# A gated mix of attention and a feed-forward block: the input loaded plainly and turned on TensorE, and more zero products

## The chip, the cores and the metric

The kernel runs on one core of a Trainium2 chip. The metric is the device time of one execution in microseconds; the kernel before takes 845.47 us, the median of three runs (844.47 to 847.02). Engines are named as in the profile: PE is TensorE, DVE is VectorE, ACT is ScalarE, POOL is GpSimd, SP is the engine whose queue issues most transfers.

## The reference

The input x is 2048 rows of 512 columns in bfloat16. A gate g is computed for each row; the output mixes an attention block with 32 heads of 16 columns and a feed-forward block of width 1792.

```python
x = A_x                                            # (1, 2048, 512)
g = sigmoid((x * gate_w).sum(-1, keepdims=True))
# a: multi-head attention without a mask
qkv = (x @ A_wqkv)                                 # 32 heads, 16 columns each
p = softmax(q @ k.T * 16 ** -0.5)
a = (p @ v) @ A_wo
# b: feed-forward
b = (silu(x @ B_w_gate) * (x @ B_w_up)) @ B_w_down
return g * a + (1 - g) * b
```

Each product contracts over the 512 columns of x, and TensorE contracts over partitions. So the kernel needs x with its columns on the partitions: the tile `xT`, 128 partitions by 4 column blocks (`dc`) by 2048 rows.

## The kernel before

The kernel has a prologue and a body. The prologue brings in x and the first weights and makes the keys, queries and a bound on the scores for the first four heads (group 0). The body runs 32 units (4 blocks of 512 queries times 8 groups of 4 heads), and each unit goes over 16 blocks of 128 keys: scores on TensorE into PSUM (`s_t`), exponentials on ScalarE (`e_t`), products with the values on TensorE (`o_ps`). A part of the exponentials (`d_t`, `y_t`, `z_t`, `u_t`) is computed on VectorE instead. The feed-forward pieces and the remaining projections are put between the scores by a planner that runs when the kernel is built. It keeps estimated clocks for the engines (`plan.pe`, `plan.dve`, `plan.act`) and fixes the order of instructions on each engine.

The load of x, in two halves of rows and four column blocks, by transfers that transpose:

```python
xT = big.tile([P, DC, S], BF16, name="xT")
for t0 in (0, 2 * QBW):                            # QBW = 512
    for dc in range(DC):                           # DC = 4
        nc.sync.dma_start_transpose(out=xT[:, dc, t0:t0 + 2 * QBW],
                                    in_=x[t0:t0 + 2 * QBW, dc * P:(dc + 1) * P])
# ... the small weight slices for group 0 on ScalarE's queue, the rest of wqkv behind x on SP's
```

The prologue proper. `keep_warm` multiplies a zero tile, so that TensorE is active while it waits for data; `k0` makes keys of group 0, `v0` values, `qp0` holds queries, `largest` takes the largest magnitude of a row (for the bound), and `k0_evict` moves the keys to SBUF:

```python
keep_warm(14)
for dc in range(DC):
    for tb in range(2):
        k0(dc, tb)
    mm(qp0[:, :], lhsT=wpad[0][:, dc, :], rhs=xT[:, dc, 0:QBW], ...)
    if dc < DC - 1:
        keep_warm(2)
largest(0, kp0[0][:, :])
act(out=q0r[:, :], in_=qp0[:, :], func=ACT.Copy)
act(out=aq0[:, :], in_=qp0[:, :], func=ACT.Abs)
vec.tensor_scalar(out=kneg1, ...)                  # bound step
for v in range(2):
    vec.tensor_scalar(out=q0[0][:, v, :], in0=q0r[:, :], ...)
k0_evict(0)
for dc in range(DC - 1):
    for tb in (2, 3):
        k0(dc, tb)
    if dc == 0:
        v0(0)
    else:
        keep_warm(3)
# ... the last k0 of each block, largest(1), largest(2), two bound steps (kneg0)
k0_evict(1)
v0(8)
mm(bp0[:, :], lhsT=kneg0, rhs=aq0[:, :], start=True, stop=True)
for v in range(2):                                 # queries with their bound; then the first scores
    vec.scalar_tensor_tensor(out=q0[0][:, v, :], in0=bp0[:, :], ...)
```

In the body, where the planner sees that TensorE would have to wait for a score bank, it first tries real work. If there is none, more than 0.4 us is left, and little work was planned in the last 3 us, it puts in four zero products, which add zeros to the accumulator that is open:

```python
if room > 0.4 and closed in o_of and 0 < pvs[closed] < KT - 1 and sum(
        w for t, w in work_at[-24:] if t > plan.pe - 3.0) < 6.5:
    for j in range(4):
        mm(o_of[closed][32 * j:32 * j + 16, :], lhsT=vaug[:, 0, G * 4 * VC:],   # a block of zeros
           rhs=xT[:, 0, 0:QBW], start=False, stop=False, tile_position=(0, 32 * j), ...)
    spend("C", 1)
    continue
```

Of the kernel before, what the change touches and what calls it, by code (L numbers as in the profile page):

```python
# [78 lines left out]
def kernel(  # L79
# [12 lines left out]
    nc = tc.nc  # L92
    P = 128
    x = A_x.flatten_outer_dims()
    S, D = x.shape
# [34 lines left out]
    const = ctx.enter_context(tc.tile_pool(name="const", bufs=1))  # L130
    big = ctx.enter_context(tc.tile_pool(name="big", bufs=1))
# [7 lines left out]
    ps_o = ctx.enter_context(tc.tile_pool(name="ps_o", bufs=1, space=bass.MemoryType.PSUM))  # L139
    ps_m = [ctx.enter_context(tc.tile_pool(name=f"ps_m{i}", bufs=1, space=bass.MemoryType.PSUM)) for i in range(3)]  # L140
# [15 lines left out]
    def mm(*args, **kw):  # L156
        return ordered(nc.tensor.matmul(*args, **kw))  # L157

    def act(*args, **kw):
        ordered(nc.scalar.activation(*args, **kw))  # L160
# [7 lines left out]
    vec = Ordered()  # L168


    xT = big.tile([P, DC, S], BF16, name="xT")
    for t0 in (0, 2 * QBW):
        for dc in range(DC):
            nc.sync.dma_start_transpose(out=xT[:, dc, t0:t0 + 2 * QBW], in_=x[t0:t0 + 2 * QBW, dc * P:(dc + 1) * P])
    wqk = big.tile([P, DC, 2 * D], BF16, name="wqk")
    for c0 in (D, 0):

        nc.scalar.dma_start(out=wqk[:, :, c0:c0 + 64],
                            in_=A_wqkv[:, c0:c0 + 64].rearrange("(dc p) c -> p dc c", p=P))
# [6 lines left out]
    for c0 in (D, 0):  # L186
        nc.sync.dma_start(out=wqk[:, :, c0 + 64:c0 + D],
                          in_=A_wqkv[:, c0 + 64:c0 + D].rearrange("(dc p) c -> p dc c", p=P))
# [1 line left out]
    wo_t = big.tile([P, NB, D], BF16, name="wo_t")  # L190

    wo_l = big.tile([P, 2, D], BF16, name="wo_l")
    wd_t = big.tile([P, FC, D], BF16, name="wd_t")

    def late_loads():
        nc.sync.dma_start(out=gw_col[:], in_=gate_w.rearrange("(dc p) -> p dc", p=P))
# [9 lines left out]

    kaug = big.tile([P, G, S], BF16, name="kaug")

    mt = big.tile([P, FC, QBW], BF16, name="mt")
    idle = mt[:, 4, :]  # L210
    nc.vector.memset(idle, 0.0)
    wpad = [mt[:, i, :].rearrange("p (dc c) -> p dc c", c=P) for i in range(2)]
# [7 lines left out]
    vsel = const.tile([P, 2], F32, name="vsel")  # L220
# [3 lines left out]
    bsel0 = mt[:, 3, 0:P]  # L224
# [3 lines left out]
    for i in (1, 0):  # L228
        nc.vector.tensor_copy(
            out=wpad[i][:, :, :].rearrange("p dc (j c) -> p dc j c", c=32)[:, :, :, 1:1 + DH],  # L230
            in_=wqk[:, :, i * D:i * D + 64].rearrange("p dc (j c) -> p dc j c", c=DH))
    def ones_rows(engine, g):

        engine.memset(kaug[:, g, :].bitcast(F32), 1.0019378662109375)
    for g in range(1, 4):
        ones_rows(nc.vector, g)
    vaug = big.tile([P, KT, G * 4 * VC + 16], BF16, name="vaug")
    nc.gpsimd.memset(vaug[:, :, G * 4 * VC:], 0.0)

# [20 lines left out]
    nc.gpsimd.memset(sel_t[:], 0.0)  # L260
    for j in range(4):
        nc.gpsimd.memset(sel_t[32 * j:32 * j + 1, j:j + 1], 1.0)
    ident = const.tile([P, P], BF16, name="ident")
    nc.gpsimd.memset(ident[:], 1.0)
    nc.gpsimd.affine_select(out=ident[:], in_=ident[:], pattern=[[-1, P]], compare_op=ALU.is_equal,
                            fill=0.0, base=0, channel_multiplier=1)

    kb = const.tile([P, NB], F32, name="kb")
    kneg = const.tile([P, NB, 8], BF16, name="kneg")
# [13 lines left out]
    plan = Plan()  # L283
    owed = []
    work_at = []
# [157 lines left out]
    def v0(t0):  # L443

        p = m_tile("vp")
        for i in range(8):
            for dc in range(DC):
                mm(p[:, 64 * i:64 * i + 64], lhsT=xT[:, dc, (t0 + i) * P:(t0 + i + 1) * P], rhs=wv[:, dc, 0:64],
                   start=(dc == 0), stop=(dc == DC - 1))
        act(out=vaug[:, t0:t0 + 8, 0:4 * VC].rearrange("p t (h c) -> p t h c", c=VC)[:, :, :, 1:1 + DH],  # L450
            in_=p[:, :].rearrange("p (t h c) -> p t h c", h=4, c=DH), func=ACT.Copy)
        m_free(p, 0.0)
# [26 lines left out]
    q1 = big.tile([P, 2, QBW], BF16, name="q1")  # L479
    nc.gpsimd.memset(q1[:], 0.0)  # L480
    nc.gpsimd.memset(qx[0][:], 0.0)
    for g in range(5, G):
        ones_rows(nc.gpsimd, g)

    q0 = [(qx[1][:, :, :, :], on_t[0][:, :, :].rearrange("p (v i) q -> p v i q", v=2))[qb // 2][:, :, qb % 2, :]
          for qb in range(QB)]
# [479 lines left out]
    kp0 = [ps_s.tile([P, 2 * QBW], F32, tag="s", name="kp0") for _ in range(2)]  # L966
    qp0 = m_tile("qp0")
# [15 lines left out]
    kneg1 = mt[:, 3, 2 * P:3 * P]  # L983

    def largest(i, ps):
        vec.tensor_reduce(out=kpart0[:, i:i + 1], in_=ps, axis=AX.X, op=ALU.max, apply_absolute_value=True)

    def k0_evict(i):
        act(out=kaug[:, 0, i * 2 * QBW:(i + 1) * 2 * QBW], in_=kp0[i][:, :], func=ACT.Identity,
            bias=onescol[:, 0:1], scale=1.0)  # L990

    keep_warm(14)
    for dc in range(DC):
        for tb in range(2):
            k0(dc, tb)
        mm(qp0[:, :], lhsT=wpad[0][:, dc, :], rhs=xT[:, dc, 0:QBW], start=(dc == 0), stop=(dc == DC - 1))
        if dc < DC - 1:
            keep_warm(2)
    largest(0, kp0[0][:, :])
    act(out=q0r[:, :], in_=qp0[:, :], func=ACT.Copy)  # L1000
    act(out=aq0[:, :], in_=qp0[:, :], func=ACT.Abs)
    vec.tensor_scalar(out=kneg1, in0=bsel0, scalar1=kpart0[:, 0:1], scalar2=None, op0=ALU.mult)
    for v in range(2):
        vec.tensor_scalar(out=q0[0][:, v, :], in0=q0r[:, :], scalar1=vsel[:, v:v + 1], scalar2=None, op0=ALU.mult)
    k0_evict(0)
    for dc in range(DC - 1):
        for tb in (2, 3):
            k0(dc, tb)
        if dc == 0:
            v0(0)  # L1010
        else:
            keep_warm(3)
    ones_rows(vec, 4)
    k0(DC - 1, 2)
    largest(1, kp0[1][:, 0:QBW])
    vec.scalar_tensor_tensor(out=kneg0, in0=bsel0, scalar=kpart0[:, 1:2], in1=kneg1, op0=ALU.mult, op1=ALU.min)
    k0(DC - 1, 3)
    largest(2, kp0[1][:, QBW:2 * QBW])
    vec.scalar_tensor_tensor(out=kneg0, in0=bsel0, scalar=kpart0[:, 2:3], in1=kneg0, op0=ALU.mult, op1=ALU.min)
    k0_evict(1)  # L1020
    v0(8)
    bp0 = m_tile("bp0")
# [2 lines left out]
    for v in range(2):  # L1025
# [5 lines left out]
                            op0=ALU.is_gt, op1=ALU.mult)  # L1031
# [268 lines left out]
    while au < UNITS:  # L1300
        if plan.slot < au * KT + at_ * KT // hi[au]:
            begin(plan.slot + 1)
            continue
        fill_dve()
        flush_act(plan.pe)
        back = pairs[0] - min(e_left.values(), default=pairs[0])
        if back >= EB - 1:
            next_pv()
            continue
        room = s_end[pairs[0] % 2] - plan.pe  # L1310
        if room > 0.02:
            if want_d():
                emit_d()
                continue
            n_pv = pv_list(plan.pe)
            switch = 0.0 if plan.mode == "C" else 0.1
            fits = int((room + SLACK - switch) / 0.216)
            c = side(room + SLACK)
            if n_pv and fits > 0 and (plan.mode == "C" or len(n_pv) > 1 and fits > 1 and (pv_turn[0] or c is None)
                                      or back >= EB - 4 or c is None and fits == 1):  # L1320
                emit_pv(n_pv[0])
                pv_turn[0] = False
                continue
            if c is not None:
                put_piece(c)
                pv_turn[0] = True
                continue
            if room > 0.4 and closed in o_of and 0 < pvs[closed] < KT - 1 and sum(
                    w for t, w in work_at[-24:] if t > plan.pe - 3.0) < 6.5:

                for j in range(4):
                    mm(o_of[closed][32 * j:32 * j + 16, :], lhsT=vaug[:, 0, G * 4 * VC:], rhs=xT[:, 0, 0:QBW],
                       start=False, stop=False, tile_position=(0, 32 * j), skip_group_check=True)
                spend("C", 1)
                continue
# [98 lines left out]
```

## Time and profile before

| | |
|---|---|
| time, median of 3 | 845.47 us (844.47 to 847.02) |
| span of the profiled execution | 843.2 us |
| exponentials on ScalarE (`e_t`, 128x1024) | 846 in 791.9 us |
| score evaluations for VectorE's exponentials (`y_t` from `d_t`, 128x512) | 356 in 234.4 us |
| mean granted TensorE clock | 0.995 |

The page gives busy time by engine, then groups of instructions. A group's line names the source line, engine and operation, then output and input tile with their shapes, the count, and after the bars the busy time, the mean of one, and the idle time of the engine just before. Where a helper issues all matmuls, all have one line (L157), so they are told apart by their tiles. A wait is read as: engine and line, what released it, us in total, how often, and the longest. In the timeline each row is a start, a length, an engine and an operation, with the idle time before it in brackets.

### The profile page before, as it was taken

To read this page: it belongs to the slowest core of one execution; us is meant where nothing else is said; L and a number is where in the kernel's file an instruction comes from. 1 tells how busy PE (TensorE), PEld (TensorE's weight loads), DVE (VectorE), ACT (ScalarE), POOL (GpSimd) and SP (SyncE) were. 2 spreads that over 40 slices of the span, in tenths; PEclk is the share of its full clock that TensorE was granted. 3 is DMA by queue.
4 is the path that set the end of the run, shared out by engine and by line. 5 is a ranking of instruction groups with operands and counts; after the bars stand their busy time and mean duration, and the time that the engine had idled before them with its cause. 6 is when DMAs were issued, how large, how long until landed. Compare 5 with 4: busy or idle time off the path is not lost. (4 is left out here: it accounts for less than half of the span.)

```text
span 843.2 us, 16224 instructions
## 1 busy us (share of the span) xinstructions
PE 763.7 (91%) x6047; PEld 263.8 (31%) x6076; DVE 795.7 (94%) x1159; ACT 815.1 (97%) x912; POOL 93.2 (11%) x122
## 2 busy tenths in 40 slices
PE   8999998999888998989889988899899898988997
PEld 3222233332332332222223323223333233332332
DVE  5999998999999999999999898999998999999996
ACT  3999999999999999999999999999999999999996
POOL 5010100010011010111010100100100110111000
PEclk9999999999999999999999999999999999999999
DMA  9432445245454334544443354454442464354232
GB/s 204 127 64 51 83 82 113 61 95 110 95 105 96 79 68 105 108 106 99 95 97 81 77 117 87 84 110 93 98 91 55 89 124 96 76 118 97 57 69 51
DMA packets 101416, 78.23 MB, mean 93 GB/s; under 512 B 77761, under 2 KB 89625, under 8 KB 101337
## 3 DMA queue, kind: packets, MB, share of 16 engines
q0 software_dynamic: 12672, 46.14, 28.7%
q1 hardware_dynamic: 86792, 30.60, 15.5%
q8 instruction: 47, 0.77, 0.4%
q10 hardware_dynamic: 1872, 0.46, 0.2%
q14 instruction: 33, 0.26, 0.1%
HBM read 20.83 MB, written 2.34 MB: 27 GB/s over the span
## 5 line engine op out<-in xcount | busy, mean ns | idle before, releaser
L160 ACT ACTIVATE e_t<-s_t 128x1024 bf16<-128x1024 f32 x846 | 791.9, 1103 | 8.2 <-PE s_t L157 6.2
L157 PE MATMUL s_t<-qx,kaug 64*128 64x512 bf16 x1376 | 293.8, 382 | 36.3 <-ACT e_t L160 31.2
L166 DVE TENSOR_SCALAR y_t<-d_t 128x512 uint16<-128x512 f32 x356 | 234.4, 680 | 16.4 <-PE d_t L157 13.5
L157 PEld LDWEIGHTS <-kaug 64*128 64x128 bf16 x2048 | 137.4, 93 | 324.1 <-issue 288.2
L157 PE MATMUL o_ps<-e_t,vaug 128*32 128x512 bf16 x1692 | 159.9, 389 | 1.5 <-DVE osb L166 1.0
L157 PE MATMUL gu_a<-xT,wg 64*128 64x512 bf16 x448 | 135.7, 377 | 0.0
L157 PE MATMUL gu_b<-xT,wu 64*128 64x512 bf16 x448 | 134.6, 377 | 1.2 <-DVE y_t L166 0.9
L157 PE MATMUL d_t<-qx,kaug 64*128 64x512 bf16 x288 | 107.6, 379 | 17.1 <-DVE y_t L166 10.3
L157 PEld LDWEIGHTS <-vaug 128*32 128x32 bf16 (+1 forms) x2132 | 45.6, 93 | 146.1 <-issue 144.8
L778 POOL DMA_DIRECT2D y_t<-u_t x44 | 40.1, 912 | 352.1 <-PE s_t L157 182.3
L778 POOL DMA_DIRECT2D y_t<-kaug x38 | 36.0, 946 | 309.7 <-PE s_t L157 199.7
L157 PE MATMUL dps_b<-wd_t,mt 64*128 64x512 bf16 x224 | 65.0, 375 | 0.3 <-DVE y_t L166 0.2
L157 PE MATMUL dps_a<-wd_t,mt 64*128 64x512 bf16 x224 | 64.9, 376 | 0.0
L166 DVE TENSOR_SCALAR z_t<-y_t 128x2048 uint16<-128x2048 uint16 x89 | 61.4, 690 | 2.1
L166 DVE TENSOR_SCALAR y_t<-y_t 128x2048 uint16<-128x2048 uint16 x89 | 60.8, 683 | 0.7 <-DMA y_t<-kaug 0.5
L166 DVE TENSOR_TENSOR u_t<-u_t 128x2048 f16<-128x2048 f16 x44 | 53.8, 1222 | 1.1
L166 DVE TENSOR_TENSOR u_t<-u_t,z_t 128x2048 f16<-128x2048 f16 x44 | 53.5, 1215 | 0.1
L157 PE MATMUL s_t<-q,kaug 64*128 64x512 bf16 x212 | 43.1, 381 | 7.6 <-ACT e_t L160 7.1
L166 DVE TENSOR_TENSOR kaug<-kaug 128x2048 f16<-128x2048 f16 x39 | 47.7, 1223 | 0.9
L157 PEld LDWEIGHTS <-wg 64*128 64x128 bf16 x448 | 41.3, 94 | 20.0 <-issue 7.7
L166 DVE TENSOR_TENSOR kaug<-kaug,z_t 128x2048 f16<-128x2048 f16 x39 | 47.4, 1216 | 0.1
L157 PEld LDWEIGHTS <-wu 64*128 64x128 bf16 x448 | 41.8, 94 | 14.7 <-issue 0.2
(131 smaller groups left out, 632.5 us busy)
## 6 DMA issues: line engine op xcount, KB each, us to landing
y_t<-u_t POOLq DMA_DIRECT2D x44, 512.0 KB, 4.8
y_t<-kaug POOLq DMA_DIRECT2D x38, 512.0 KB, 4.9
wg<-in_B_w_gate_dram SPq DMA_DIRECT2D x56, 128.0 KB
wu<-in_B_w_up_dram SPq DMA_DIRECT2D x56, 128.0 KB
y_t<-wd_t POOLq DMA_DIRECT2D x6, 512.0 KB, 4.6
on<-osb SPq DMA_DIRECT2D x120, 16.0 KB
rb<-rr SPq DMA_DIRECT2D x15, 128.0 KB
wd_t<-in_B_w_down_dram SPq DMA_DIRECT2D x7, 256.0 KB
```

Of the source, the lines that this page charges most:

```text
L157: return ordered(nc.tensor.matmul(*args, **kw))
L160: ordered(nc.scalar.activation(*args, **kw))
L166: return lambda *a, **kw: ordered(f(*a, **kw))
L778: nc.gpsimd.dma_start(out=ya, in_=ua, accum_op=ALU.add)
```

## The change

Two things are changed together. First, x is loaded row by row as it lies in memory, in four blocks of 512 rows, into tiles that are not yet in use, and turned on TensorE: a product with the identity puts each 128x128 block into PSUM with its columns on the partitions, and VectorE or ScalarE copies it to `xT`. The prologue is rearranged by block of 512 rows, with fewer products for warmth. The identity is made earlier, and the fills of `kaug` with ones go from VectorE to GpSimd. It is meant to replace the transposing transfers by plain ones, with TensorE doing useful work early. Second, the planner's threshold for zero products rises from 6.5 to 8.5, which is meant to keep TensorE's clock up in stretches with little work.

```diff
-    for t0 in (0, 2 * QBW):
-        for dc in range(DC):
-            nc.sync.dma_start_transpose(out=xT[:, dc, t0:t0 + 2 * QBW], in_=x[t0:t0 + 2 * QBW, dc * P:(dc + 1) * P])
+    x_rows = [wd_t[:, TQ * b:TQ * b + TQ, :] for b in range(QB - 1)] + [mt[:, 8:8 + TQ, :]]
+    for b in range(QB):
+        nc.sync.dma_start(out=x_rows[b], in_=x[b * QBW:(b + 1) * QBW, :].rearrange("(i p) d -> p i d", p=P))
...
-    for g in range(1, 4):
-        ones_rows(nc.vector, g)
+    ident = const.tile([P, P], BF16, name="ident")          # moved up
...
-    for g in range(5, G):
+    for g in range(1, G):
         ones_rows(nc.gpsimd, g)
...
-    keep_warm(14)
-    ... (the prologue shown above)
+    def turn(b, dc):
+        i = len(tps) % 3
+        tps.append((ps_m[1].tile([P, QBW], F32, tag="m1", name="tp") if i == 0 else
+                    ps_m[2].tile([P, QBW], F32, tag="m2", name="tp") if i == 1 else
+                    ps_o.tile([P, QBW], F32, tag="o", name="tp")))
+        tp = tps[-1]
+        for k in range(TQ):
+            mm(tp[:, k * P:(k + 1) * P], lhsT=x_rows[b][:, k, dc * P:(dc + 1) * P], rhs=ident[:, :],
+               start=True, stop=True)
+        dst = xT[:, dc, b * QBW:(b + 1) * QBW]
+        if dc % 2 or dc and b in (1, 2):
+            act(out=dst, in_=tp[:, :], func=ACT.Copy)
+        else:
+            vec.tensor_copy(out=dst, in_=tp[:, :])
+
+    keep_warm(8)
+    for b in range(QB):
+        for dc in range(DC):
+            turn(b, dc)
+        if b == 2:
             v0(0)
+        for dc in range(DC):
+            k0(dc, b)
+            if b == 0:
+                mm(qp0[:, :], lhsT=wpad[0][:, dc, :], rhs=xT[:, dc, 0:QBW], start=(dc == 0), stop=(dc == DC - 1))
+        if b == 0:
+            act(out=q0r[:, :], in_=qp0[:, :], func=ACT.Copy)
+            act(out=aq0[:, :], in_=qp0[:, :], func=ACT.Abs)
+        elif b == 1:
+            largest(0, kp0[0][:, :])
+            vec.tensor_scalar(out=kneg1, in0=bsel0, scalar1=kpart0[:, 0:1], scalar2=None, op0=ALU.mult)
+            k0_evict(0)
+            for v in range(2):
+                vec.tensor_scalar(out=q0[0][:, v, :], in0=q0r[:, :], scalar1=vsel[:, v:v + 1], scalar2=None, op0=ALU.mult)
         else:
-    ...
+            largest(b - 1, kp0[1][:, (b - 2) * QBW:(b - 1) * QBW])
+            vec.scalar_tensor_tensor(out=kneg0, ...)
     k0_evict(1)
     v0(8)
...
             if room > 0.4 and closed in o_of and 0 < pvs[closed] < KT - 1 and sum(
-                    w for t, w in work_at[-24:] if t > plan.pe - 3.0) < 6.5:
+                    w for t, w in work_at[-24:] if t > plan.pe - 3.0) < 8.5:
```

More of the change, by code (lines that the diff above doesn't have):

```diff
@@ L171 @@
     xT = big.tile([P, DC, S], BF16, name="xT")
-    for t0 in (0, 2 * QBW):
-        for dc in range(DC):
-            nc.sync.dma_start_transpose(out=xT[:, dc, t0:t0 + 2 * QBW], in_=x[t0:t0 + 2 * QBW, dc * P:(dc + 1) * P])
+    wd_t = big.tile([P, FC, D], BF16, name="wd_t")
+    mt = big.tile([P, FC, QBW], BF16, name="mt")
+    x_rows = [wd_t[:, TQ * b:TQ * b + TQ, :] for b in range(QB - 1)] + [mt[:, 8:8 + TQ, :]]
+    for b in range(QB):
+        nc.sync.dma_start(out=x_rows[b], in_=x[b * QBW:(b + 1) * QBW, :].rearrange("(i p) d -> p i d", p=P))
     wqk = big.tile([P, DC, 2 * D], BF16, name="wqk")
@@ L192 @@
     wo_l = big.tile([P, 2, D], BF16, name="wo_l")
-    wd_t = big.tile([P, FC, D], BF16, name="wd_t")
     def late_loads():
@@ L207 @@
     kaug = big.tile([P, G, S], BF16, name="kaug")
-    mt = big.tile([P, FC, QBW], BF16, name="mt")
     idle = mt[:, 4, :]
@@ L234, in ones_rows @@
         engine.memset(kaug[:, g, :].bitcast(F32), 1.0019378662109375)
-    for g in range(1, 4):
-        ones_rows(nc.vector, g)
+    ident = const.tile([P, P], BF16, name="ident")
+    nc.gpsimd.memset(ident[:], 1.0)
+    nc.gpsimd.affine_select(out=ident[:], in_=ident[:], pattern=[[-1, P]], compare_op=ALU.is_equal,
+                            fill=0.0, base=0, channel_multiplier=1)
     vaug = big.tile([P, KT, G * 4 * VC + 16], BF16, name="vaug")
@@ L262 @@
         nc.gpsimd.memset(sel_t[32 * j:32 * j + 1, j:j + 1], 1.0)
[L263 to L266, printed above, removed]
     kb = const.tile([P, NB], F32, name="kb")
@@ L990, in k0_evict @@
             bias=onescol[:, 0:1], scale=1.0)
-    keep_warm(14)
[L993 to L1009, printed above, removed]
-            v0(0)
-        else:
[L1012 to L1016, printed above, removed]
@@ L1017 @@
-    k0(DC - 1, 3)
-    largest(2, kp0[1][:, QBW:2 * QBW])
-    vec.scalar_tensor_tensor(out=kneg0, in0=bsel0, scalar=kpart0[:, 2:3], in1=kneg0, op0=ALU.mult, op1=ALU.min)
+    tps = []
+    def turn(b, dc):
[12 more added lines that the diff above has]
+            vec.tensor_copy(out=dst, in_=tp[:, :])
@@ new lines @@
+    keep_warm(8)
[3 more added lines that the diff above has]
+        if b == 2:
+            v0(0)
+        for dc in range(DC):
[11 more added lines that the diff above has]
+                vec.tensor_scalar(out=q0[0][:, v, :], in0=q0r[:, :], scalar1=vsel[:, v:v + 1], scalar2=None, op0=ALU.mult)
+        else:
+            largest(b - 1, kp0[1][:, (b - 2) * QBW:(b - 1) * QBW])
+            vec.scalar_tensor_tensor(out=kneg0, in0=bsel0, scalar=kpart0[:, b - 1:b], in1=(kneg1, kneg0)[b - 2],
+                                     op0=ALU.mult, op1=ALU.min)
```

## The prediction

> **What bounds the kernel now.** I read the page's first part first: busy time by engine.
>
> ```profile
> PE 763.7 (91%) x6047; PEld 263.8 (31%) x6076; DVE 795.7 (94%) x1159; ACT 815.1 (97%) x912; POOL 93.2 (11%) x122
> ```
>
> ScalarE (ACT) is nearly full, but 97% is an average, so I asked where its idle time lies: the list of waits (engine, waiting line, what it waited for; us in all, times, longest).
>
> ```profile
> PE s_t L157 <- ACT e_t L160: 39.2, 120, 0.9
> ...
> ACT q0r L160 <- PE qp L157: 7.1, 1, 7.1
> ACT e_t L160 <- PE s_t L157: 6.2, 13, 1.5
> ACT mt L160 <- PE a_l_b L157: 3.8, 1, 3.8
> ACT kaug L160 <- DVE kpart L166: 3.4, 1, 3.4
> ```
>
> TensorE's score matmuls wait for the exponentials 120 times; the exponentials wait for scores 13 times, 6.2 us in all. So in the body ScalarE sets the pace and TensorE has slack. The span splits into three: time before the first exponential, the stream of exponentials, and the tail. The timeline places the first exponential at 18.83 us and the end of the last at 834.81 (the last group starts at 825.43 and lasts 9.38), leaving 8.4 us of tail. Between 23.34, where the stream becomes continuous, and 835, I summed ScalarE's waits by stretch of 100 us: about 5.5 us. That is all the body can win, 0.65% of the span.
>
> Next, what ends the prologue. The timeline (start us, length us, engine, operation):
>
> ```profile
> 6.68 0.59 PE L157 MATMUL kp<-xT,mt 128*128 128x512 bf16 x2
> ...
> 14.88 0.69 DVE L166 TENSOR_REDUCE kpart<-kp 128x1 f32<-128x512 f32 x1 [1.22 <-PE kp L157]
> ...
> 16.03 0.69 DVE L166 TENSOR_REDUCE kpart<-kp 128x1 f32<-128x512 f32 x1
> 16.76 1.11 ACT L160 ACTIVATE kaug<-kp,onescol 128x1024 bf16<-128x1024 f32 x1 [3.35 <-DVE kpart L166]
> ...
> 17.17 0.39 PE L157 MATMUL bp<-aq,mt 128*128 128x512 bf16 x1 [0.24 <-DVE mt L166]
> ...
> 18.83 2.98 ACT L160 ACTIVATE e_t<-s_t 128x1024 bf16<-128x1024 f32 x3 [0.47 <-PE s_t L157]
> ```
>
> The path is k products, the last row maximum (16.03), the bound product (17.17), first scores, first exponential: 2.8 us from the start of the last maximum to the first exponential. The change leaves these 2.8 us alone and moves what stands before them.
>
> Last, the granted clock. In 5 us windows of the body it is below full in only two places:
>
> ```profile
> 255.00:260.00 5.00, 4.89 (x34) 1.43 (x34) 4.89 (x8) 4.24 (x5) 0.35 (x1) 0.66 0.60 122
> 545.00:550.00 5.00, 3.95 (x24) 1.41 (x25) 5.00 (x9) 4.86 (x6) 0.86 (x1) 0.88 1.03 184
> 550.00:555.00 5.00, 5.00 (x41) 1.47 (x38) 4.50 (x7) 3.73 (x5) 0.00 (x0) 0.77 0.31 62
> ```
>
> The columns after the window are its length, busy us of PE, PEld, DVE, ACT and POOL (instructions in brackets), then the clock: 0.66, 0.88 and 0.77. In finer windows it is 0.50 from about 255.35 to 258.7 and again from about 548.6 to 552.1, some 3.4 us each. In the 3.4 us ahead of the first dip the timeline shows about 5.5 array passes of 0.216 us, in those ahead of the second about 7: 35% and 44% of the time. ScalarE loses 0.8 us in the first dip and 1.4 us in the second: 2.2 us.
>
> **What the Trainium skill says.** "TensorE: Matmul & The Clock Gate", Part 1 (the HAM clock gate): the clock halves after a free-running window of about 3.4 us with too little activity and returns after a busy one. The trace agrees: two dips of about 3.4 us, each after a sparse stretch, and matmuls of 0.62 instead of 0.38 us inside. It also starts cold: the first warm-up products have a spacing of 0.427 us, then 0.216 from about 6.2 us. Same page, Part 4 (PE-mode transpose): a turned block lands in PSUM and must be copied to SBUF. No turned block is in the trace before, but copies of that size are: 128x512 PSUM to SBUF takes VectorE 0.68 us (row of y_t) and ScalarE 0.59. "DMA: Bandwidth & Descriptors", Latency and other measured facts: a transposing DMA reaches 261 GB/s where source rows aren't contiguous. The trace shows 145 to 286 GB/s while the transposes run (2 to 11 us) and 341 to 354 in the plain loads at 15 to 18 us. So plain loads do move faster.
>
> **Part 1, the prologue.** Removed: eight transposing DMAs (issued from 0.81 to 12.05 us), 18 of 26 warm-up products and four fills of kaug on VectorE (0.91 us each, in idle time). Added: four plain loads of 512 KB, 64 products of 128x128 and 16 copies of 128x512 out of PSUM (6 VectorE, 10 ScalarE).
>
> Data first. Bytes flow from about 2 us. 512 KB at about 165 GB/s (the trace's 2 to 5 us, with the same small weight loads alongside) is 3.2 us: block 0 lands near 5.2. The other three at about 200 GB/s land near 7.8, 10.4 and 13; below they are never waited for. The eight warm-up products end at 4.7.
>
> The rest is the order of the built instructions. Three banks carry four turned tiles per block, so tile 3 waits for the copy of tile 0, and TensorE is in order. I use copy 0.68 on VectorE, 0.55 from start to start on ScalarE, 0.3 for a tile of four products (estimated from 32 weight-load and product pairs in 1.2 us, widened to 128 columns; 0.45 while cold), 0.216 for a k or q product.
> - Block 0: tiles from 5.2; tile 0 copied by 6.55, tile 3 turned at 6.6 and copied by 7.7; four k and four q products end at 8.8.
> - Block 1: ScalarE first does q0r and aq0 (8.8 to 9.95), then three copies (0.55 apart, last done 11.55); k products end at 12.0.
> - VectorE then takes the maximum over 1024 columns (1.22), kneg1 0.25 and q0 0.61, to 14.1, before tile 0 of block 2, done 14.8. ScalarE waits for the maximum at 13.25, evicts k (1.1), then copies. Block 2's tile 3 needs the bank of its tile 0: copied by 16.0. The v products (1.1) start at 15.1, the four k products at 16.2; they end at 17.2.
> - Block 3: the maximum and bound step end at 18.3, two VectorE copies at 18.95 and 19.6, tile 3 turned at 19.0 and copied by 20.1; k products end at 20.5.
>
> The last maximum starts at 20.55 and not at 16.03; with 2.8 us the first exponential is at 23.4: +4.5 us. TensorE is sparse from 10 to 15 us, near or below the 35 to 44% of the two dips, so a clock drop there is more likely than not. It would double the 2.0 us of v and k products of block 2; at 0.5 chance, +1. Against it, hand-over waits and copies may be shorter than I took them; -1. I keep +4.5.
>
> All of it is on the path: no exponential can run earlier, and their count is the same 846.
>
> **Part 2, zero products.** The threshold 6.5 to 8.5 raises the zero products in the order from 84 to 396: 78 more groups of four. Four run side by side in one pass of 0.216 us: 17 us of TensorE in all. They are planned only where the score bank has 0.4 us to wait, and TensorE waits for exponentials 39.2 us already, so most is hidden. I allow 0.6 us for those that delay a score (ScalarE lost 5.5 us over 846 exponentials with TensorE less full). Gain: if both dips go, 2.2 us; I count three quarters, 1.6. The planner also reshuffles feed-forward pieces; all product and exponential counts of real work stay equal, so I give that nothing.
>
> Sum: 845.5 + 4.5 - 1.6 + 0.6 = **849.0 us**, 0.4% slower.
>
> **Rivals.**
> - The load was the limit: for it, the second half of k products is strung out to 15.6 us with VectorE and TensorE waiting, and plain loads are faster. If turning were never waited for, all x is there at 13 us and the first exponential might come at 17 us: -2, time about 842. Against it: 16 copies plus the maxima alternate with three banks on in-order engines.
> - The zero products cure more than the dips, say all 5.5 us of body waits: time about 845. Against it: at 125 to 130 us ScalarE loses 0.8 us at full clock.
> - TensorE becomes the bound: it is at 91% busy and gains 17 us. If a third lands on the path, +5.6: 855. Against it: 120 waits for exponentials, and the placement in planned gaps.
>
> **Range and chances.** The prologue term runs from +2 to +7, the body from -4 to +2; combined not at their extremes, 845 to 854. Two per cent is 17 us, which no rival reaches: within 2% 0.96, faster 0.01, slower 0.03.
>
> **What would show it.** Right: first exponential between 22 and 25 us with the last maximum 2.8 us before it; copies of tp standing between the k products; ScalarE's body waits down by 1 to 2 us; the dips gone from the body; TensorE busy up by some 10 to 17 us. Wrong: a first exponential before 20 us (copies cheaper or overlapped), block 0 landing after 7 us (then worse still), waits of e_t for zero products, or dips that stay.

## The result and the profile after

The changed kernel takes 865.07 us, the median of four runs (863.78 to 865.89), against 844.97 us for the kernel before (843.68 to 847.02). The ratio is 1.0234, with a 95% interval of 1.0209 to 1.0259: slower by over 2%, where 849 was predicted and 845 to 854 was the range.

The first part of the page (busy time by engine) and the waits of ScalarE, in the changed kernel:

```profile
PE 780.6 (90%) x6406; PEld 268.3 (31%) x6434; DVE 802.4 (93%) x1161; ACT 821.0 (95%) x922; POOL 95.8 (11%) x126
```

```profile
ACT xT L160 <- PE tp L157: 14.7, 4, 9.6
ACT e_t L160 <- PE s_t L157: 10.6, 17, 3.5
```

TensorE is busy 17 us longer, inside the 10 to 17 that were expected. Two things stand out in the waits. ScalarE waited 9.6 us in one piece for a turned tile (`tp`), and the waits of exponentials for scores, which were to shrink, grew from 6.2 to 10.6 us, with one of 3.5 us among them; the longest was 1.5.

Where the 19.8 us between the two spans (843.2 and 863.0) lie is read from the stream of exponentials:

| | before | after | difference |
|---|---|---|---|
| start of the first exponential | 18.83 | 34.76 | +15.9 |
| from there to the end of the last | 816.0 | 819.6 | +3.6 |
| tail | 8.4 | 8.6 | +0.2 |

So four fifths of the loss are in the prologue. Its timeline in the changed kernel (start, length, engine and operation, with the idle time before in brackets):

```profile
5.34 1.02 PE L157 MATMUL tp<-ident,wd_t 128*128 128x128 bf16 x12 [0.49 <-POOL vaug L243]
...
7.55 1.81 POOL L479 MEMSET qx<- 128x2048 bf16 x1
...
7.74 7.94 DVE L229 COPY mt<-wqk 128x256 bf16<-128x256 bf16 x1 [1.30 <-DMA wqk<-in_A_wqkv_dram]
7.89 7.80 DVE L166 CAST xT<-tp 128x512 bf16<-128x512 f32 x2
9.29 6.29 POOL L234 MEMSET kaug<- 128x1024 f32 x7
...
15.76 0.58 PE L157 MATMUL tp<-ident,wd_t 128*128 128x128 bf16 x4 [9.40 <-DVE xT L166]
...
31.97 0.69 DVE L166 TENSOR_REDUCE kpart<-kp 128x1 f32<-128x512 f32 x1 [0.94 <-PE kp L157]
...
34.76 2.98 ACT L160 ACTIVATE e_t<-s_t 128x1024 bf16<-128x1024 f32 x3 [0.47 <-PE s_t L157]
```

The rows of block 0 are there at 5.34 and three tiles are turned by 6.4. Then TensorE waits 9.40 us for a copy by VectorE. VectorE isn't idle by the profile: it is "busy" for 7.94 us with one copy of 128x256 bfloat16, a piece of the small weights, which took 0.26 us in the kernel before:

```profile
3.60 0.30 DVE L229 COPY mt<-wqk 128x256 bf16<-128x256 bf16 x1 [0.68 <-DMA wqk<-in_A_wqkv_dram]
5.53 0.26 DVE L229 COPY mt<-wqk 128x256 bf16<-128x256 bf16 x1 [1.62 <-DMA wqk<-in_A_wqkv_dram]
```

Its end, 15.68, is 0.1 us after the end of GpSimd's seven fills of `kaug` (9.29 + 6.29 = 15.58). The turned tiles (CAST) stand in VectorE's queue behind it. What comes after the last maximum takes the 2.8 us that it took before.

The second loss is in one place of the body:

```profile
117.58 2.28 DVE L166 TENSOR_REDUCE kb<-bblk 128x1 f32<-128x2048 bf16 x1
...
122.89 0.68 DVE L166 TENSOR_SCALAR y_t<-y_t 128x2048 uint16<-128x2048 uint16 x1
...
123.63 0.62 PE L157 MATMUL o_ps<-y_t,vaug 128*32 128x512 bf16 x4 [2.18 <-DVE y_t L166]
...
126.31 1.94 ACT L160 ACTIVATE e_t<-s_t 128x1024 bf16<-128x1024 f32 x2 [3.46 <-PE s_t L157]
```

TensorE's next product in order needs `y_t`, which VectorE finishes late, at 123.57. TensorE stands for 2.18 us, with the next scores behind that product, and ScalarE for 3.46. The windows show the clock there (length, busy us of PE, PEld, DVE, ACT and POOL with instructions, clock, DMA share, GB/s), and in the prologue:

```profile
10.00:15.00 5.00, 0.00 (x0) 0.00 (x0) 5.00 (x3) 0.00 (x0) 5.00 (x7) 0.50 1.11 351
15.00:20.00 5.00, 4.24 (x22) 2.10 (x22) 0.78 (x4) 0.91 (x2) 0.58 (x1) 0.56 0.57 145
...
120.00:125.00 5.00, 1.41 (x8) 0.39 (x8) 4.27 (x7) 2.84 (x4) 0.86 (x1) 0.68 0.29 52
125.00:130.00 5.00, 4.96 (x29) 1.01 (x28) 2.15 (x4) 2.83 (x3) 0.00 (x0) 0.64 0.50 100
```

The clock is at half after the long wait, and the eight k and q products of block 0 stand 0.43 us apart instead of 0.216. In the stall at 120 to 130 it is at half again for a part of the time (0.68 and 0.64 in the two windows of 5 us), and after 130 us this profile has no drop: the two of the kernel before are gone.

### The profile page after: what moved, and what is told of

It is laid out like the page before. It is cut to its first block, busy times and chain, and to the rows that moved or that the text cites. A ratio compares the mean times of both kernels' runs of the same rounds, so it can differ in the third digit from the quotient of the medians.

```text
span 863.0 us, 16960 instructions
## 1 busy us (share of the span) xinstructions
PE 780.6 (90%) x6406; PEld 268.3 (31%) x6434; DVE 802.4 (93%) x1161; ACT 821.0 (95%) x922; POOL 95.8 (11%) x126
## 5 line engine op out<-in xcount | busy, mean ns | idle before, releaser
L160 ACT ACTIVATE e_t<-s_t 128x1024 bf16<-128x1024 f32 x846 | 792.2, 1093 | 11.4 <-PE s_t L157 10.6
L157 PE MATMUL s_t<-qx,kaug 64*128 64x512 bf16 x1372 | 292.6, 382 | 26.2 <-ACT e_t L160 20.0
L166 DVE TENSOR_SCALAR y_t<-d_t 128x512 uint16<-128x512 f32 x356 | 234.7, 680 | 17.4 <-PE d_t L157 15.6
L157 PEld LDWEIGHTS <-kaug 64*128 64x128 bf16 x2048 | 130.6, 93 | 305.9 <-issue 268.5
L157 PE MATMUL d_t<-qx,kaug 64*128 64x512 bf16 x292 | 109.0, 378 | 13.1 <-DVE y_t L166 6.4
L157 PEld LDWEIGHTS <-vaug 128*32 128x32 bf16 (+1 forms) x2444 | 49.5, 93 | 163.3 <-issue 160.6
L776 POOL DMA_DIRECT2D y_t<-kaug x37 | 33.1, 896 | 284.3 <-PE s_t L157 129.2
```

The lines of the kernel that those rows point to most:

```text
L166: return lambda *a, **kw: ordered(f(*a, **kw))
L776: nc.gpsimd.dma_start(out=ya, in_=ua, accum_op=ALU.add)
```

## The experiments

Two parts were changed together, so there are two questions. For the prologue: does GpSimd's filling hold VectorE's copy (the first explanation), or is it a late load, or the turning itself? For the body: are the added zero products in the way, or the order that the planner makes of everything else once its threshold is another?

### The seven fills, held back and doubled

The fills (and what GpSimd has to do ahead of them) wait here for VectorE's second weight copy. No work is left out:

```diff
-            nc.vector.tensor_copy(out=wpad[i]...)
+            padded = nc.vector.tensor_copy(out=wpad[i]...)
...
-    nc.gpsimd.memset(q1[:], 0.0)
+    held_fill = nc.gpsimd.memset(q1[:], 0.0)      # and a dependency of held_fill on padded
```

> The changed kernel, but GpSimd's large fills (q1, qx, kaug) start only after VectorE's two copies of the small weights. Theory A (VectorE's copy stood still for 7.9 us because GpSimd's back-to-back fills held what the two engines share): the second weight copy takes 0.3 us instead of 7.94, the first turned tile is copied near 8.5 us instead of 15.7, TensorE's clock does not fall at 10 us, the first exponential comes at 24 to 26 us instead of 34.8, and the time is 854 to 857 us. Rival B (the copy waits for data or for busy transfers): nothing changes, 863 to 866 us. Rival C (copies out of PSUM are held up by fills as well): the two copies of turned tiles are now the ones that stand still, first exponential above 32 us, time above 861.

Measured: 863.03 us (861.51 to 864.95), ratio 1.0217 (1.0194 to 1.0240); first exponential at 29.48, 5.3 us earlier than in the changed kernel. Its timeline:

```profile
8.29 0.26 DVE L229 COPY mt<-wqk 128x256 bf16<-128x256 bf16 x1 [2.50 <-DMA wqk<-in_A_wqkv_dram]
...
12.39 6.29 POOL L234 MEMSET kaug<- 128x1024 f32 x7
12.92 0.69 DVE L166 CAST xT<-tp 128x512 bf16<-128x512 f32 x1 [3.21 <-PE tp L157]
15.51 1.22 DVE L166 TENSOR_REDUCE kpart<-kp 128x1 f32<-128x1024 f32 x1 [1.90 <-PE kp L157]
...
16.77 1.96 DVE L166 TENSOR_SCALAR mt<-mt,kpart 128x128 bf16<-128x128 bf16 x1
16.94 2.18 DVE L166 TENSOR_SCALAR qx<-q0r,vsel 128x512 bf16<-128x512 bf16 x2
```

The copy is 0.26 us again, so neither its shape nor the loads beside it are the cause. The first exponential and the time are nevertheless short of what theory A expected, and the clock falls at 10.0 us here too. The fills now run later and hold two other operations: the bound step (0.25 us before) and the queries (0.61) end at 18.73 and 19.12, again when the fills end (18.68). While the same fills run, a copy and a maximum out of PSUM take their usual 0.69 and 1.22. So of the operations seen here those are held that read bfloat16 from SBUF and write it to SBUF, and not those whose source is PSUM; which of these properties decides was not tried.

Doubling the dose: the seven fills are issued twice.

```diff
     for g in range(1, G):
         ones_rows(nc.gpsimd, g)
+    for g in range(1, G):
+        ones_rows(nc.gpsimd, g)
```

> The changed kernel with GpSimd's seven fills of kaug issued twice (14 instead of 7, same values). Theory A: VectorE's second weight copy lasts 6.3 us longer, 14.2 us instead of 7.94, the first exponential comes near 41 us and the time is 870 to 873 us. Rival B (the copy waits for data or transfers): the copy still ends at 15.7 us, time 863 to 866 us. If instead the copy may go in between two fills as soon as one is complete, the length also stays at 7.9 us or less.

Measured: 876.24 us, first exponential at 40.79.

```profile
8.07 13.83 DVE L229 COPY mt<-wqk 128x256 bf16<-128x256 bf16 x1 [1.63 <-DMA wqk<-in_A_wqkv_dram]
...
9.29 12.51 POOL L234 MEMSET kaug<- 128x1024 f32 x14
```

6.22 us more of fills make the copy 5.89 us longer and the first exponential 6.0 us later; the copy ends at 21.90, the fills at 21.80. That settles who holds whom. This one execution is 11.5 us longer than the profiled one of the changed kernel (864.75), and not 6: the other 5.5 us are in the body (825.1 against 819.6), of which more below.

### Does GpSimd give way between two fills?

Here each fill of `kaug` overlaps the one ahead by one element, so it has to wait until that one has been written. The values written are the same.

```diff
     for g in range(1, G):
-        ones_rows(nc.gpsimd, g)
+        lo = 2 if g > 1 else 0
+        nc.gpsimd.memset(kaug...[:, g * S - lo:(g + 1) * S], ...)     # the last pair of the group before too
```

> The changed kernel, but each of GpSimd's six later fills of kaug waits until the fill before it is complete (each overlaps it by one element of four bytes). Theory A1 (VectorE's copy gets in only when GpSimd has to wait): the second weight copy ends at 9.4 to 10.5 us, after the fill of qx and at most one fill of kaug, 1.5 to 2.5 us long instead of 7.9; first exponential at 28 to 31 us, time 859 to 863 us. Theory A2 (one long hold, whatever GpSimd waits for): copy still 7 to 8 us, first exponential near 35, time 864 to 867.

```profile
7.56 1.81 POOL L479 MEMSET qx<- 128x2048 bf16 x1
8.26 2.12 DVE L229 COPY mt<-wqk 128x256 bf16<-128x256 bf16 x1 [1.80 <-DMA wqk<-in_A_wqkv_dram]
...
9.30 7.03 POOL L483 MEMSET kaug<- 128x1024 f32 x7
...
28.42 2.98 ACT L160 ACTIVATE e_t<-s_t 128x1024 bf16<-128x1024 f32 x3 [0.47 <-PE s_t L157]
```

The copy is held until 10.38, that is through the fill of `qx` and one of `kaug` (7.03/7 = 1.0 us each), and not through seven. So back-to-back fills keep VectorE out as one, and a wait between two of them lets it in; the waits cost GpSimd 0.7 us in all. The first exponential comes at 28.42, 6.3 us earlier than in the changed kernel. The one time is nevertheless 865.37 us, which alone would speak for theory A2: the body took 826.6 us, and the length of the copy is what decides between the two.

### The fills alone, on the kernel before

The same seven fills on GpSimd, with x loaded as before, nothing turned, threshold 6.5.

```diff
-    for g in range(1, 4):
-        ones_rows(nc.vector, g)
...
-    ones_rows(vec, 4)
...
-    for g in range(5, G):
+    for g in range(1, G):
         ones_rows(nc.gpsimd, g)
```

> The kernel before with one thing of the change alone: all seven fills of kaug go to GpSimd. They then run from 9 to 15.5 us, and VectorE's bound step (0.25 us) and its two products for the queries (0.6 us), which start at 11.8 us and read and write SBUF alone, fall into them. Theory A: these operations end near 15.5 us, the last maximum starts 0.5 to 1.5 us later, first exponential 19.3 to 20.5 us, time 845.5 to 847. Rival B (fills hold up nothing; the copy of the changed kernel waited for data): first exponential 18.8 us, none of these operations longer than 0.7 us, time as before.

Measured: 845.54 us against 844.56 beside it, ratio 1.0005 (0.9988 to 1.0021).

```profile
9.17 6.30 POOL L234 MEMSET kaug<- 128x1024 f32 x7
10.44 1.23 DVE L166 TENSOR_REDUCE kpart<-kp 128x1 f32<-128x1024 f32 x1 [4.96 <-PE kp L157]
11.70 3.82 DVE L166 TENSOR_SCALAR mt<-mt,kpart 128x128 bf16<-128x128 bf16 x1
11.87 4.04 DVE L166 TENSOR_SCALAR qx<-q0r,vsel 128x512 bf16<-128x512 bf16 x2
```

The hold is there too (3.82 us for 0.25), so turning isn't needed for it, but here it costs the first exponential 0.94 us (19.77) and the time nothing that can be measured: most of the hold fell into time in which VectorE, in the kernel before, was idle or had a fill of its own to do (12.5 to 14.9). In the kernel before, GpSimd's last fill ended at 11.90 and the bound step started at 11.81; it was free by a hair.

### Each part alone

Turning alone is the changed kernel with the threshold at 6.5; zero products alone is the kernel before with 8.5.

```diff
-                    w for t, w in work_at[-24:] if t > plan.pe - 3.0) < 8.5:      # turning alone
+                    w for t, w in work_at[-24:] if t > plan.pe - 3.0) < 6.5:
...
-                    w for t, w in work_at[-24:] if t > plan.pe - 3.0) < 6.5:      # zero products alone
+                    w for t, w in work_at[-24:] if t > plan.pe - 3.0) < 8.5:
```

> The loading and turning of the input alone: the threshold for zero products is back at 6.5. Theory A: the prologue carries nearly all of the loss, first exponential at 34 to 36 us as in the changed kernel; from first to last exponential 815 to 818 us as in the kernel before (816.0), time 860 to 862 us. Rival D (the zero products carry a third or more of the loss): the time falls below 858 us. Rival E (the body got slower because of the prologue, not of the threshold): body of 819 to 820 us, time 864 to 866.

> The higher threshold alone, 8.5, on the kernel before. What the prediction took: 843.5 to 845, the two clock drops at 255 and 549 us gone, body 1 to 2 us shorter. Theory from the changed kernel's body (819.6 us against 816.0): 847 to 849.5 us, with a stretch in which ScalarE waits for TensorE behind VectorE. Rival D: above 850.

Turning alone: 861.75 us (861.28 to 862.13), ratio 1.0201 (1.0181 to 1.0222); first exponential at 34.46, body 816.5, so 15.6 of its 16.4 us are prologue. Zero products alone: 848.34 us (848.04 to 851.68), ratio 1.0051 (1.0030 to 1.0073); first exponential at 18.83, body 819.3. The two losses, 16.4 and 3.0, add up to 19.5 of the 20.1 us. So the threshold didn't gain 1 us, it lost 3. In the body of the kernel with zero products alone the two drops at 255 and 549 us are gone, but there is one at 487, around which ScalarE loses 1.25 us. Zero products alone has the stall of the changed kernel too, at about the same distance from its first exponential (it ends 90.2 us after it at 109.03, and 91.6 after it in the changed kernel at 126.31):

```profile
30.66 0.39 PE L157 MATMUL o_ps<-xT,vaug 128*16 128x512 bf16 x4
...
100.31 2.28 DVE L166 TENSOR_REDUCE kb<-bblk 128x1 f32<-128x2048 bf16 x1
...
105.62 0.69 DVE L166 TENSOR_SCALAR y_t<-y_t 128x2048 uint16<-128x2048 uint16 x1
...
106.36 0.62 PE L157 MATMUL o_ps<-y_t,vaug 128*32 128x512 bf16 x4 [2.20 <-DVE y_t L166]
...
109.03 1.94 ACT L160 ACTIVATE e_t<-s_t 128x1024 bf16<-128x1024 f32 x2 [3.48 <-PE s_t L157]
```

The first of these lines is the only group of zero products ahead of the stall: four of them, 0.39 us long and 75 us earlier. So it isn't their time that stops ScalarE at 106 us. They moved the planner's clock, and from 35.84 us on VectorE's instructions stand in another order than in the kernel before. There, on the same stretch:

```profile
98.21 15.81 ACT L160 ACTIVATE e_t<-s_t 128x1024 bf16<-128x1024 f32 x17
...
106.72 2.27 DVE L166 TENSOR_REDUCE kb<-bblk 128x1 f32<-128x2048 bf16 x1
```

The same maximum `kb` starts at 106.72 and not at 100.31, after another `y_t` has been made and the accumulator copied, and ScalarE runs on without a wait. With the wait that follows (0.95), the stall costs 4.4 us.

### The turning, mended

Both mendings of the fills together, and the threshold at 6.5.

```diff
     (the changed kernel, with: fills held until the weight copy, each fill waiting for the one ahead)
-                    w for t, w in work_at[-24:] if t > plan.pe - 3.0) < 8.5:
+                    w for t, w in work_at[-24:] if t > plan.pe - 3.0) < 6.5:
```

> Loading and turning alone (threshold 6.5), GpSimd's large fills after VectorE's weight copies and then one by one. If the hold by the fills was the only thing the prediction lacked in the prologue: no VectorE operation of the prologue longer than 1.3 us, first exponential 23.5 to 26 us (predicted 23.4, plus 2.0 to 2.5 us for the later small weights), body 815 to 818, time 850 to 854 us. If half-clock stretches cost more than the 1 us I allowed: first exponential 26.5 to 29 us, time 853 to 857.

Measured: 855.59 us (854.50 to 856.92), ratio 1.0126 (1.0103 to 1.0149); first exponential at 29.24.

```profile
8.19 0.26 DVE L229 COPY mt<-wqk 128x256 bf16<-128x256 bf16 x1 [2.45 <-DMA wqk<-in_A_wqkv_dram]
...
17.39 0.98 DVE L166 TENSOR_SCALAR mt<-mt,kpart 128x128 bf16<-128x128 bf16 x1
17.56 1.98 DVE L166 TENSOR_SCALAR qx<-q0r,vsel 128x512 bf16<-128x512 bf16 x2
```

Still 10.4 us later than before, and 5.8 later than the 23.4 of the prediction; the time is in the range that was expected if stretches at half clock cost more. The second piece of the small weights is there at 8.19 and not at 5.53: it travels beside the plain loads, which keep the DMA engines full (a share of 1.14 at 5 to 10 us in the changed kernel); that these delay it was not tried by itself. Tile 3 of block 0 is therefore turned at 9.07 instead of the predicted 6.6. The products of block 0 end at 13.07, 4.0 us later instead of 2.2, as the clock is at half. The bound step and the queries are still held for a part of a fill each time, and with that and another stretch at half clock block 2 takes 7.1 us instead of 5.2. So this is not a prologue without a hold, and none was run. The earliest first exponential of all is that of the fills one by one without the delay, 28.42; their hold of the copy ends 1.9 us after the copy could have ended (8.26 + 0.26), which puts it at some 26.6 without that hold, an estimate and still 7.7 us later than in the kernel before.

### Where in the body the threshold costs and where it gains

A unit takes some 25.5 us (816 us for 32), so the stall falls in the fourth unit and the first clock drop of the kernel before in the tenth. So the threshold was raised only once six units are closed, and only before that, both on the kernel before:

```diff
-                    w for t, w in work_at[-24:] if t > plan.pe - 3.0) < 6.5:
+                    w for t, w in work_at[-24:] if t > plan.pe - 3.0) < (8.5 if closed >= 6 else 6.5):   # late
...
+                    w for t, w in work_at[-24:] if t > plan.pe - 3.0) < (8.5 if closed < 6 else 6.5):    # early
```

> The kernel before with threshold 8.5 from unit 6 on and 6.5 ahead of it, so that the order of the first 170 us stays as before. Theory F (the threshold's loss is one stall of some 4.5 us at 104 to 110 us, which comes from the reshuffled order): no such stall, time 842 to 846 us. Theory G (the added zero products cost time wherever they are): 847 to 849 us.

> The kernel before with threshold 8.5 ahead of unit 6 alone and 6.5 after. Theory F: the stall of 4 to 5 us at 104 to 110 us is there with only 32 zero products more than before; time 847.5 to 850 us. Theory G: no more than 845.5 us, as only a tenth of the added products is left.

Late: 841.77 us, the median of ten runs (841.13 to 843.65), ratio 0.9964 (0.9953 to 0.9975). It is faster than both kernels. Its body takes 812.9 us, the clock is 0.999, and the waits of the exponentials for scores fell from 6.2 to 3.7 us:

```profile
ACT e_t L160 <- PE s_t L157: 3.7, 8, 1.5
```

Added up over the timeline from the first exponential on, ScalarE waits 4.1 us instead of 7.1. The waits that are gone are those at the two drops of the kernel before (2.0 us), one of 0.75 at 814 us and one of 0.3 at 397.

Early: 853.31 us (853.01 to 854.41), ratio 1.0101 (1.0076 to 1.0125), slower than the full threshold. Its profile has the stall (ScalarE loses 4.5 us at 110 to 120) and a second loss, a clock at half from 25 to 35 us, in which ScalarE loses 3.1 us. The same kernel once more, on another chip:

> The kernel before with threshold 8.5 ahead of unit 6, once more. In its first profile the clock was at half from 24.8 to 34.6 us, which cost ScalarE some 3 us more than the stall of 4.9 us that was expected. If this belongs to the program, it is there again and the time is 853 to 854.5 us; if it was the chance of one execution, the stretch is at full clock and the time is 848 to 851 us.

It took 848.88 us, with the stall at 105 to 115, but at full clock from 25 to 35. So the stall comes with this order of instructions, and the drop at 25 to 35 need not. It wasn't the chance of one execution either: all four runs on the first chip took some 853 us, at a mean clock of 0.985 to 0.987 against 0.993 here. Why isn't settled.

### The products without the new order

To part the products from the order, the kernel before got 99 more groups of four zero products at places where its planner waits, without its clocks being moved: all real work keeps its order (VectorE's and ScalarE's instructions are the same, one by one, in both traces).

```diff
+            if room > 0.4 and closed in o_of and 0 < pvs[closed] < KT - 1 and sum(
+                    w for t, w in work_at[-24:] + unplanned[-24:] if t > plan.pe - 3.0) < 8.5:
+                for j in range(4):
+                    mm(o_of[closed][32 * j:32 * j + 16, :], lhsT=vaug[:, 0, G * 4 * VC:], rhs=xT[:, 0, 0:QBW], ...)
+                unplanned.append((plan.pe, 1))
             if room > 0.15:
                 plan.pe += 0.1
                 continue
```

> The kernel before with 99 more groups of four zero products, put in where the threshold 8.5 allows it but without moving the planner's clocks, so that the order of all real work on all engines is that of the kernel before. Theory F (the early stall comes from the reshuffled order, the products themselves help): no stall near 105 us, both clock drops gone or fewer, body 812 to 815 us, time 841 to 844. Theory G (zero products cost time themselves): ScalarE's waits for scores go up, time 846 to 850.

Measured: 845.48 us, the median of twenty runs, against 844.56 (31 runs); ratio 1.0015 (0.9999 to 1.0030). No stall, with sixteen zero products ahead of 110 us where the kernel with the stall has four, and no drop where the kernel before has its two:

```profile
255.00:260.00 5.00, 5.00 (x47) 1.75 (x45) 4.90 (x8) 5.00 (x6) 0.15 (x1) 1.00 0.59 119
395.00:400.00 5.00, 4.38 (x32) 1.22 (x31) 5.00 (x10) 3.70 (x5) 0.00 (x0) 1.00 0.54 118
...
550.00:555.00 5.00, 5.00 (x49) 1.39 (x46) 4.93 (x8) 4.89 (x7) 0.00 (x0) 1.00 0.26 52
```

And yet nothing is gained, which neither theory had: the body is 816.1 us, as before. ScalarE now loses 1.3 us at 395 to 400 at full clock, and another wait has grown. The first fence is the kernel before, the second this one:

```profile
ACT e_t L160 <- PE o_ps L157: 0.5, 2, 0.3
```

```profile
ACT e_t L160 <- PE s_t L157: 5.2, 13, 1.5
ACT e_t L160 <- PE o_ps L157: 1.5, 2, 1.3
```

Ahead of that wait VectorE stands 1.69 us for a transfer (`y_t<-kaug`), which took 6.54 us here and 4.79 in the kernel before; no zero product stands between 376 and 402 us. Whether the transfer is late because of the added products or by chance was not tried.

So the products as such don't make the stall; the new order does. Nor is a gain of theirs seen in the time by themselves: the drops that they cure are worth 2.0 us, and most of that is lost again in one wait. With the late threshold both are gone, the drops and some waits at full clock (814 and 397 us), but the order of its later units is another too; which step of that matters was not isolated.

### The changed kernel once more

With the fills held, doubled or one by one the body came out longer than in the changed kernel (822.4, 825.1 and 826.6 against 819.6), although all three differ from it in nothing but GpSimd's fills. A second profile of the changed kernel, unedited, on another chip:

> The changed kernel once more, to see whether the clock drops of its body fall at the same places in a second execution. If the places are set by the program: half clock near 10 to 19, 25 to 28, 42 and 122 to 127 us again and nowhere after 130 us; 863 to 866 us. If they are set by a window that runs on its own: the stretches that follow from a long wait (10 us, 122 us) again, the others elsewhere.

863.75 us; first exponential at 33.73, and the stall again, 3.0 us at 120 to 125 and 1.0 after it. The drop in block 2 (26.2 to 29.6 us in the first profile) isn't there, and block 2 takes 4.9 us instead of 6.0, which is the 1.0 us by which the first exponential is earlier. The clock drops elsewhere: at 575 to 580 (ScalarE loses 1.4 us), where the first profile is at full clock:

```profile
15.00:20.00 5.00, 4.24 (x17) 2.04 (x17) 0.68 (x3) 0.80 (x2) 0.57 (x1) 1.00 0.55 143
...
575.00:580.00 5.00, 3.43 (x16) 0.67 (x14) 4.85 (x7) 3.62 (x5) 0.82 (x1) 0.70 0.92 168
```

The windows of the kernel with held fills (first fence) and of the changed kernel in its first profile (second) show the same at two places:

```profile
570.00:575.00 5.00, 3.43 (x22) 0.64 (x17) 4.96 (x7) 3.99 (x6) 0.67 (x1) 0.82 0.80 141
...
700.00:705.00 5.00, 3.30 (x20) 0.67 (x17) 4.70 (x9) 3.38 (x4) 0.86 (x1) 0.79 0.56 110
```

```profile
575.00:580.00 5.00, 3.28 (x28) 1.26 (x26) 4.90 (x8) 4.96 (x6) 1.17 (x1) 1.00 0.57 92
...
705.00:710.00 5.00, 3.80 (x31) 0.94 (x29) 4.93 (x9) 4.68 (x6) 0.56 (x1) 1.00 0.57 112
```

Counted from the first exponential these are the same stretches of work, some 545 and 675 us in. Both kernels are thin there (TensorE busy 3.3 to 3.8 of 5 us), and the clock drops in one execution and not in the other. The kernel with held fills loses 4.0 us at 570 to 580 and 700 to 710, the changed kernel under 1 us in the same work. That is about the 2.8 us by which its body is longer (822.4 against 819.6), and so the 5.3 us won in its prologue show as 2.0 in the time. The two others with a long body have drops at these stretches as well and at a third, some 725 us in; the one with the fills one by one has two more, at 375 and 498 us. How often a drop falls where was not counted. So the body of one profile can be 3 to 7 us longer than that of another in this order of instructions, and differences of a few us between single profiles say nothing by themselves.

## Why the prediction was wrong

**Block 0: "tile 0 copied by 6.55".** This is the step that failed. Set against the predicted times, in the timelines:

| | predicted | changed kernel | mended, threshold 6.5 |
|---|---|---|---|
| block 0 lands | 5.2 | 5.3 | 5.3 |
| tile 3 turned | 6.6 | 15.76 | 9.07 |
| k and q products of block 0 end | 8.8 | 19.7 | 13.1 |
| k products of block 1 end | 12.0 | 22.7 | 16.1 |
| k products of block 2 end | 17.2 | 28.7 | 23.2 |
| k products of block 3 end | 20.5 | 31.9 | 26.4 |
| first exponential | 23.4 | 34.8 | 29.2 |

Of the 11.4 us that the prologue is later than predicted, 9.2 arise before tile 3 of block 0: some 2.0 by the later small weights (the next paragraph) and some 7.1 by the hold, if tile 3 follows the start of the second weight copy by 0.88 us as it does with held fills (8.29 and 9.17; the split is an estimate). The path had no such wait in it. The sum counted what the fills leave on VectorE ("four fills of kaug on VectorE (0.91 us each, in idle time)") and nothing of what they do from GpSimd. The Trainium skill has it: "SBUF — State Buffer", SBUF: two separate sides, says that GpSimd and VectorE share a pair of ports under an exclusive lock, and Who interferes with whom says which VectorE operations take it: copies and multiplications by a scalar in their fast modes, not reductions. The trace agrees on the kinds (7.94 us for a copy, 3.82 for a multiplication, 1.22 as ever for a maximum), though the maximum here reads PSUM, so that kind and source are not told apart. It differs in the length: the page gives the pair for one instruction, and here VectorE was kept out through seven issued back to back (through fourteen in the doubled run), and let in after one only where GpSimd had to wait between them. That these ports are the means is the page's account; the runs show that the fills hold VectorE, when, and which operations.

**The small weights** were left out of "the order of the built instructions". The mended kernel shows this term by itself: tile 0's copy on VectorE stands behind the second weight copy, whose piece came at 8.2 and not at 5.5, and tile 3 was turned 2.5 us later than worked out.

**"A clock drop there is more likely than not … +1".** The mechanism was right. In block 2, where it was expected, a drop came in the first profile and not in the second; with it the block took 6.0 us and without it 4.9, so it costs 1.1 and not 2.0. What was missing is the drop in block 0, which comes after the long wait and makes the stretch of its eight products 1.7 us longer. What stood against it ("hand-over waits and copies may be shorter than I took them; -1") came to little: blocks 1 and 3 took 0.2 and 0.1 us less than worked out.

**What held.** The data of block 0 landed within 0.1 us of the estimate; the steps of blocks 1 and 3 and the 2.8 us at the end are right; TensorE's 17 us are right. So is the sign of the prologue's term: even mended, turning is slower here than the transposing loads, 855.59 us against 845.27.

**"The planner also reshuffles feed-forward pieces; … so I give that nothing".** This failed as well. The same counts in another order cost a stall of 4.4 us, where TensorE stands behind a product for which VectorE is late. The body was predicted 1.0 us shorter and is 3.6 longer. The gain was named rightly: more products do take away the two drops (full clock at 255 and 550), and these are worth 2.0 us, near the 2.2 that were read. Whether it shows in the time depends on the order of the rest: with the late threshold 3.5 us are won, with the products alone nothing that can be measured. No trace shows what the products cost by delaying a score, so the "0.6 us" stays untested.

**The rivals.** The load of x was not the limit: block 0 was there at 5.34, and no later block was waited for. TensorE is not the bound: it waits for exponentials 26.9 us still. That the products cure more than the drops is so with the late threshold alone (3.0 us of waits), and by the order that comes with it. None of the three had another engine's fills in it, which is why the range, built from the listed terms, was too narrow.

## What to carry to other kernels

Work moved to GpSimd isn't free because it is off the path: ask what VectorE does from SBUF to SBUF in that time, and let the fills wait between one another, which shortened the hold from 7.94 to 2.12 us here. When a change moves a planner's threshold, compare the order of each in-order engine, since counts and busy times can stay and a single late operand still stops three engines; raising it only after the first six units, and so keeping the order ahead of them, gave 841.77 us, the best time of this study. And an operation that takes thirty times its usual length, as the weight copy did (7.94 us for 0.26), was waiting here, although the profile called it busy.

## What the runs showed of the hardware that was not expected

- GpSimd fills issued back to back kept VectorE's SBUF-to-SBUF operations out as one block: 7.94 us for seven fills, 13.83 for fourteen, 2.12 where each fill waited for the one ahead. Copies and maxima out of PSUM ran at their usual 0.69 and 1.22 us meanwhile.
- The profile books this as busy time of VectorE: from 7.74 to 15.69 us without a gap, for a copy and two casts that take 0.26 + 1.28 us elsewhere.
- The clock drops of TensorE in thin stretches fall in some executions and not in others, with the same instructions: at 575 us in the second profile of the changed kernel and not in the first.
- The recorded clock can miss a drop. In the second profile of the changed kernel it reads 1.00 from 15 to 20 us, while the k and q products stand 0.43 us apart, as in the first profile at a recorded 0.56.
- Small loads beside plain loads of 512 KB came later than beside transposing ones: the second piece of the weights at 7.7 to 8.3 us instead of 5.5. No run tells what delays them.
